# Linear attention, mixture of experts and a squared-ReLU layer on one core: one two-bank tile for the whole kernel, or for the attention stage alone

## The chip, the cores and the metric

The kernel runs on 1 core of one Trainium2 chip. The metric is the device time of one execution in microseconds (us): median 1135.84 over 3 runs (1135.78 to 1138.93). The engines of the core work side by side, each through its own list of instructions in order: PE (TensorE, matmuls; its weight loads are listed as PEld), DVE (VectorE), ACT (ScalarE), POOL (GpSimd) and SP (SyncE, which here only issues DMAs). Where an instruction needs what another engine makes or still reads, it waits for a semaphore, and everything behind it on its own engine waits too.

## The reference

Three layers in a row, on 4 x 576 = 2304 tokens of 512 features:

```python
# 1. linear attention, 8 heads of 64, phi into 2 x 128 features
proj = x @ w_phi;  proj -= max|proj|;  phi = [exp(proj), exp(-proj)]
out  = (phi(q) @ (phi(k)^T v)) / (phi(q) . sum(phi(k)) + 1e-6)
# 2. mixture of 8 experts, two per token, F = 1024
noisy = x @ w_gate + log1p(exp(x @ w_noise)) * noise
y = sum over the top 2 experts e: gate_e * (relu(x @ w1[e]) @ w2[e])
# 3. last layer, F2 = 2048
out = relu(y @ w_in)**2 @ w_out
```

Matrices are multiplied in float32: each product is made of three matmuls (high x high, high x low, low x high), into one PSUM accumulator.

## The kernel before, in words

**Order.** The whole program is written out by hand (`tc.manual_schedule()`): each engine runs its instructions in the order in which the program names them. What the framework adds is the waiting: it records which instruction writes and reads which *tile* and puts a semaphore wait wherever a later one must not overtake an earlier one.

**PSUM.** PE writes into PSUM, 8 banks of 512 float32 per partition. `bank(tag, shape)` hands out a bank by name. `Tk`, `M0`, `M1`, `KV`, `N0` and `N1` are tiles of one bank each, and each call makes a new tile in the bank of that name. `Tq` and `P` are different: they are the two halves of one tile `pair` of two banks, made once at the start, and `bank("Tq")` and `bank("P")` are views of it (`PAIR = ["Tq", "P"]`). In the trace both show as `pair`.

**Attention** (to about 235 us). 36 units run as a software pipeline. `q_b` (L474 on) writes the query projection of a unit into both halves of `pair` at once and copies both out with one ACT instruction (L481); this is why the two banks are one tile. Routing of tokens runs beside it in groups: `r_3b` (L652 on) counts ranks with matmuls into a bank, in the last groups into `P`; `r_4` (L667 on) reads the ranks on DVE, `r_4b` makes the slots, and `r_5` (L742) scatters the token rows into `xg_d` by indirect DMAs from POOL's queue, ordered by expert.

**The seam** (about 235 to 268 us). The first two 128-row blocks of expert 0 ("part 0") are computed while the last routing groups finish. Its accumulators are `ACC[0]` and `ACC[1]`. The last group goes `r_3b(g)`, `e_2(0, 2)`, `r_4(g)`, `r_4b(g)`, `r_5`. When its rows have landed, three blocks `xs` of expert 0 are loaded (L167), transposed (L184), and part 1 begins.

**Experts** (to about 720 us). A part is an expert with its 640 slots (5 blocks j of 128 rows); expert 7 is cut in two parts of 2 and 3 blocks. For each of 8 slices f of F, `e_1(part, f)` makes the hidden slice in `M0` and `M1`, ACT (`hh`, L213) and DVE (`hl`, L210) split it into high and low, and `e_2(part, f)` adds it to five accumulators, one per block: `YP[j] = bank(ACC[j])` with `ACC = ["Tq", "KV", "P", "N0", "N1"]`. `e_1` of the next slice stands before `e_2` of this one. At the border of two experts the order on PE is: the transposes of the next expert's rows (`x_t`, L184) between the blocks of slice 6; slice 7 of blocks 0, 1 and 2; `e_1` of the new expert's slice 0; slice 7 of blocks 3 and 4; `e_1` of its slice 1. After a block's last matmul `e_y` (L220) copies the accumulator to SBUF on ACT and stores it. ACT also converts weights (L138) and, beside DVE and POOL, turns the float64 weights of the last layer into float32 (`wide_a`, `wide_b`, L931 to L945).

**Last layer** (to about 1124 us). Five blocks of rows, four of 4 x 128 and one (the second) of 2 x 128. The first block's rows are gathered and transposed (`l_t`, L988) into the banks `Tk`, `Tq`, `KV` and `M0` just before the last slice of expert 7; DVE and ACT take them out (L95, L96). Then 16 slices per block: `l_1` into `M0` or `M1`, ACT (L1005, L1008) and DVE (L1009, L1010) make the square and split it, `l_2` adds to `bank(ACC[j])`. At the end of a block the accumulators are copied out, j = 0 and 2 by ACT (L1029), j = 1 and 3 by DVE (L1027), and stored. A branch for overfull experts follows; it isn't taken with these inputs.

Of the kernel before, what the change touches and what calls it, by code (L numbers as in the profile page):

```python
# [9 lines left out]
FT = mybir.dt.float32  # L10
# [22 lines left out]
def kernel(  # L33
# [26 lines left out]
    DC = DM // 128  # L60
# [8 lines left out]
    psum = ctx.enter_context(tc.tile_pool(name="psum", bufs=1, space=bass.MemoryType.PSUM))  # L69
# [6 lines left out]
    x_d = dram.tile([NT, DM], FT, name="x_d")  # L76
    g_d = dram.tile([NT, E], FT, name="g_d")

    pair = psum.tile([128, 2, 512], FT, tag="pair", name="pair")

    def bank(tag, shape):
        if tag not in PAIR:
            return psum.tile(shape, FT, tag=tag, name=tag)
        names = "abc"[:len(shape) - 1]
        n = 1
        for x in shape[1:]:
            n *= x
        return pair[:, PAIR.index(tag), :n].rearrange(
            f"p ({' '.join(names)}) -> p {' '.join(names)}", **dict(zip(names, shape[1:])))
# [4 lines left out]
    def hi_lo(hi, lo, src):  # L94
        nc.scalar.activation(hi, src, AF.Copy)  # L95
        nc.vector.tensor_sub(lo, src, hi.bitcast(FT))  # L96
# [46 lines left out]

    NJ = CAP // 128
    NF = F // 128
    ACC = ["Tq", "KV", "P", "N0", "N1"]
    parts = [(0, 0, JA), (0, JA, NJ)] + [(e, 0, NJ) for e in range(1, E - 1)] + [(E - 1, 0, JA), (E - 1, JA, NJ)]
    XG, XT, HT, YP, xp = {}, {}, {}, {}, [None]

# [25 lines left out]
    def x_t(pt, j):  # L175
        e = parts[pt][0]
        if pt not in XT:
            n = RA if pt == 0 else CAP
            XT[pt] = (x_tile(pt, [128, DC, n], FR, "xth", ("kp", 2)), x_tile(pt, [128, DC, n], FR, "xtl", ("kp", 2)))
            if pt == NP - 2:  # L180
                XT[pt + 1] = XT[pt]
        t = bank(["Tk", "M0", "M1"][j % 3], [128, DC, 128])
        for d in range(DC):
            nc.tensor.transpose(t[:, d], XG[pt, j][:, d * 128:d * 128 + 128], ident)  # L184
        c = x_cols(pt, j)
        hi_lo(XT[pt][0][:, :, c], XT[pt][1][:, :, c], t)
# [3 lines left out]
    def e_1(pt, f, later=False):  # L190
        e, j0, j1 = parts[pt]
        wh, wl = wt[2 * e + f // 4, 0]
        fc = (f % 4) * 128
        xh, xl = XT[pt]
        n, x0 = (j1 - j0) * 128, x_cols(pt, j0).start
        if n <= 512:
            cut = [(bank(f"M{f % 2}", [128, n]), 0, n)]
        else:
            cut = [(bank(f"M{i}", [128, n // 2]), i * (n // 2), (i + 1) * (n // 2)) for i in range(2)]
        for d in range(DC):  # L200
            for i, (a, b) in enumerate(((wh, xh), (wh, xl), (wl, xh))):
                for o, c0, c1 in cut:
                    mm(o, a[:, d, fc:fc + 128], b[:, d, x0 + c0:x0 + c1], d == 0 and i == 0, d == DC - 1 and i == 2)
        m = RA if pt == 0 else CAP
        hh = x_tile(pt, [128, m], FR, "hh", ("kth", 2), 2)
        hl = x_tile(pt, [128, m], FR, "hl", ("ktl", 2), 2)
        HT[pt, f] = (hh, hl)

        def low(o, c0, c1):
            nc.vector.scalar_tensor_tensor(hl[:, c0:c1], o, 0.0, hh[:, c0:c1].bitcast(FT), op0=OP.max, op1=OP.subtract)  # L210

        for c in cut:
            nc.scalar.activation(hh[:, c[1]:c[2]], c[0], AF.Relu)  # L213
            if not later:
                low(*c)
        return lambda: [low(*c) for c in cut]
# [6 lines left out]
    def e_2(pt, f, js=None):  # L223
# [4 lines left out]
        for j in range(j0, j1) if js is None else js:  # L228
            if f == 0:
                YP[j] = bank(ACC[j], [128, DM])  # L230
            c = slice((j - j0) * 128, (j - j0) * 128 + 128)
# [5 lines left out]

    with ExitStack() as actx:
        xp[0] = ap_ = actx.enter_context(tc.tile_pool(name="attn", bufs=1))

        KT, KTT, VT, VTT, QT, QTT, NZ = {}, {}, {}, {}, {}, {}, {}

# [545 lines left out]
        for n in range(NU + 2):  # L788
            b, i = divmod(n, 9)
# [97 lines left out]


    wpb[0] = ctx.enter_context(tc.tile_pool(name="wpb", bufs=1))

    with ExitStack() as ectx:
        xp[0] = ep = ectx.enter_context(tc.tile_pool(name="experts", bufs=1))
# [88 lines left out]
        def l_t(m, i):  # L981
            ya, _ = YA.pop((m, i))
            if i == 0:
                X2[m] = [ep.tile([128, DC, 512], FR, name="x2", tag=x, bufs=1)
                         for x in (("xth", "xtl") if m % 2 == 0 else ("xg", "wd"))]
            t = bank("Tk" if m else ("Tk", "Tq", "KV", "M0")[i], [128, DC, 128])
            for d in range(DC):
                nc.tensor.transpose(t[:, d], ya[:, d * 128:d * 128 + 128], ident)  # L988
            c = slice(i * 128, i * 128 + 128)
            hi_lo(X2[m][0][:, :, c], X2[m][1][:, :, c], t)  # L990
# [22 lines left out]
        def l_2(u):  # L1013
# [4 lines left out]
            for j, tt in enumerate(blocks[m]):  # L1018
                if f == 0:
                    OP_[j] = bank(ACC[j], [128, DM])  # L1020
                c = slice(j * 128, j * 128 + 128)
# [114 lines left out]
        for i in range(R):  # L1136
            l_t(0, i)
        e_2(NP - 1, NF - 1)
        NU = len(blocks) * NF2
        for u in range(NU + 1):  # L1140
            m, f = divmod(u, NF2)
            if u < NU:
                l_1(u)
            if u > 0:
                l_2(u - 1)
            if m == 0 and pieces.get((NP, f)):
                ahead_load(2)
                for p in pieces[NP, f]:
                    w_conv(*p)
            if m + 1 < len(blocks):  # L1150
                if f in (3, 6, 9, 12) and f // 3 - 1 < len(blocks[m + 1]):
                    l_gather(m + 1, f // 3 - 1)
                if f in (4, 7, 10, 13) and (f - 1) // 3 - 1 < len(blocks[m + 1]):
                    l_sum(m + 1, (f - 1) // 3 - 1)
                if f in (5, 8, 11, 14) and (f - 2) // 3 - 1 < len(blocks[m + 1]):
                    l_t(m + 1, (f - 2) // 3 - 1)
# [8 lines left out]
    with tc.If(most > CAP):  # L1165
        with ExitStack() as sctx:
# [27 lines left out]
            with tc.For_i(0, NT, 128) as row:  # L1194
# [8 lines left out]
                for e in range(E):  # L1203
# [4 lines left out]
                    for f in range(F // 128):  # L1208
                        t = bank(f"M{f % 2}", [128, 128])
# [3 lines left out]
                    t = bank("P", [128, DM])  # L1213
# [5 lines left out]
                for n in range(F2 // GF):  # L1219
# [4 lines left out]
                    for f in range(GF // 128):  # L1224
                        t = bank(f"M{f % 2}", [128, 128])
# [15 lines left out]
def build(nc, inputs):  # L1241
    import numpy as _np
    import concourse.tile as _tile
    from concourse import mybir as _mybir
    arrays, args = {}, []
    for name in _INS:
        a = _np.ascontiguousarray(inputs[name])
        if a.dtype == _np.float64:
            a = a.view(_np.int64)
        arrays[f"in_{name}_dram"] = a  # L1250
        args.append(nc.dram_tensor(f"in_{name}_dram", a.shape, _mybir.dt.from_np(a.dtype), kind="ExternalInput").ap())
    for i, (shape, dtype) in enumerate(_OUTS):
        dt = _mybir.dt.from_np(_np.dtype(dtype))
        args.append(nc.dram_tensor(f"out_{i}_dram", shape, dt, kind="ExternalOutput").ap())
    with _tile.TileContext(nc) as tc:
        kernel(tc, *args)
    return arrays
# [11 lines left out]
```

## Time and profile before

| | |
|---|---|
| runs: median, lowest, highest | 1135.84, 1135.78, 1138.93 us |
| the profiled execution, and its span from first to last instruction | 1136.58 us, 1134.8 us |
| mean granted TensorE clock | 0.992 |
| busy: PE, PEld | 1095.5 us (97%), 928.2 us (82%) |
| busy: DVE, ACT, POOL | 605.0 us (53%), 478.8 us (42%), 397.6 us (35%) |
| chain that ended last | PE 73%, ACT 2%, DVE 1%, DMA 1% |
| ... by line | PE M L92 36%, PE pair L92 16%, PE N L92 12%, PE KV L92 8% |

Times in a trace count from the span's first instruction. A timeline row gives the start, the duration, the engine, the line, the operation and, as out<-in, the tiles that it writes and reads; a bracket at the end gives the time for which the engine stood idle just before and who ended that. Lines are those of the helper that issues: all matmuls of `mm` have L92, and a tile's name tells them apart. A matmul's duration includes its way through the array, so two that follow each other overlap: what one costs PE is the distance from start to start.

### The profile page before, as it was taken

To read this page: it belongs to the slowest core of one execution; us is meant where nothing else is said; L and a number is where in the kernel's file an instruction comes from. 1 tells how busy PE (TensorE), PEld (TensorE's weight loads), DVE (VectorE), ACT (ScalarE), POOL (GpSimd) and SP (SyncE) were. 2 spreads that over 40 slices of the span, in tenths; PEclk is the share of its full clock that TensorE was granted. 3 is DMA by queue.
4 is the path that set the end of the run, shared out by engine and by line. 5 is a ranking of instruction groups with operands and counts; after the bars stand their busy time and mean duration, and the time that the engine had idled before them with its cause. 6 is when DMAs were issued, how large, how long until landed. Compare 5 with 4: busy or idle time off the path is not lost.

```text
span 1134.8 us, 17634 instructions
## 1 busy us (share of the span) xinstructions
PE 1095.5 (97%) x6652; PEld 928.2 (82%) x6652; DVE 605.0 (53%) x1197; ACT 478.8 (42%) x970; POOL 397.6 (35%) x374
## 2 busy tenths in 40 slices
PE   7999899999999999999999999999999999999996
PEld 5777677698898989898898989788898888888884
DVE  4566677771277767777777773342343333333222
ACT  4666566623434444444435353442232322232221
POOL 3333444654454645454545556461020100000000
PEclk9999999999999999999999999999999999999998
DMA  5777343236564546455554655332121101001001
GB/s 136 231 193 226 95 131 112 95 132 206 169 208 154 188 159 186 171 187 186 186 195 159 208 163 161 114 107 56 38 57 38 30 26 56 19 1 38 1 1 39
DMA packets 105468, 137.77 MB, mean 121 GB/s; under 512 B 17442, under 2 KB 59554, under 8 KB 105378
## 3 DMA queue, kind: packets, MB, share of 16 engines
q1 hardware_dynamic: 99618, 117.72, 32.9%
q0 software_dynamic: 5760, 18.88, 5.1%
q8 instruction: 54, 0.88, 0.3%
q14 instruction: 36, 0.29, 0.1%
HBM read 92.97 MB, written 43.59 MB: 120 GB/s over the span
## 4 chain that ended last, share of the span: by engine, by line
PE 73%; ACT 2%; DVE 1%; DMA 1%; issue 0%; SPq 0%; ACTq 0%
PE M L92 36%; PE pair L92 16%; PE N L92 12%; PE KV L92 8%; PE M L184 1%; PE Tk L184 1%; PE Tk L988 1%; DMA xg_d<-xt,slots 0%; DMA xs<-xg_d 0%; ACT y L220 0%; ACT r L1005 0%; DVE xtl L96 0%; ACT w30h L138 0%; ACT w10h L138 0%; ACT o L1029 0%
## 5 line engine op out<-in xcount | busy, mean ns | idle before, releaser
L1009 DVE TENSOR_TENSOR r<-M,r 128x512 f32<-128x512 f32 (+1 forms) x80 | 51.1, 638 | 247.3 <-ACT h2h L1008 247.3
L213 ACT ACTIVATE hh<-M 128x320 fp32r<-128x320 f32 (+2 forms) x128 | 50.9, 437 | 233.5 <-PE M L92 233.5
L1005 ACT ACTIVATE r<-M 128x512 f32<-128x512 f32 (+1 forms) x80 | 44.4, 555 | 248.0 <-PE M L92 248.0
L210 DVE SCALAR_TENSOR_TENSOR hl<-M,hh 128x320 fp32r<-128x320 f32 (+2 forms) x128 | 58.3, 487 | 123.7 <-ACT hh L213 123.4
L483 POOL PARTITION_ALL_REDUCE qmx<-ps x36 | 69.8, 1941 | 121.4 <-ACT ps L481 100.7
L970 POOL DMA_INDIRECT ya<-y_d,yrows x18 | 18.0, 998 | 188.8 <-PE Tk L988 113.3
L92 PE MATMUL N<-kvc,qp 128*128 128x81 f32 x512 | 65.7, 283 | 5.1 <-DVE ll L519 2.5
L92 PEld LDWEIGHTS N<-kvc,qp 128*128 128x128 f32 x512 | 61.4, 197 | 10.8 <-issue 5.5
L1010 DVE TENSOR_TENSOR h2l<-r,h2h 128x512 fp32r<-128x512 f32 (+1 forms) x80 | 57.7, 721 | 7.3 <-DVE r L1009 0.5
L96 DVE TENSOR_TENSOR ktl<-Tk,kth 128x512 fp32r<-128x512 f32 (+1 forms) x38 | 25.2, 664 | 53.5 <-ACT kth L95 53.5
L1008 ACT ACTIVATE h2h<-r 128x512 fp32r<-128x512 f32 (+1 forms) x80 | 47.1, 589 | 2.6
L92 PE MATMUL M<-x,w30h 128*128 128x512 f32 (+1 forms) x160 | 45.9, 371 | 0.0
L139 POOL TENSOR_TENSOR w20l<-wstage,w20h 128x512 fp32r<-128x512 f32 x20 | 28.1, 1406 | 50.4 <-ACT w20h L138 25.5
L92 PE MATMUL M<-x,w20h 128*128 128x512 f32 (+1 forms) x160 | 45.7, 370 | 0.0
L92 PE MATMUL M<-x,w10h 128*128 128x512 f32 (+1 forms) x160 | 45.7, 370 | 0.0
L92 PE MATMUL M<-x,w00h 128*128 128x512 f32 (+1 forms) x160 | 45.4, 368 | 0.0
L139 POOL TENSOR_TENSOR w30l<-wstage,w30h 128x512 fp32r<-128x512 f32 x20 | 27.4, 1370 | 51.1 <-ACT w30h L138 50.9
L742 POOL DMA_INDIRECT xg_d<-x,slots x32 | 32.9, 1027 | 15.6 <-DVE slots L703 9.4
L139 POOL TENSOR_TENSOR w10l<-wstage,w10h 128x512 fp32r<-128x512 f32 x16 | 22.2, 1390 | 40.2 <-ACT w10h L138 37.1
L940 POOL TENSOR_TENSOR wd<-wd 128x256 f32<-128x256 f32 x32 | 23.9, 746 | 35.3 <-DVE wd L936 34.6
L940 POOL TENSOR_TENSOR wx<-wx 128x256 f32<-128x256 f32 x32 | 23.7, 741 | 35.2 <-DVE wx L936 33.8
L92 PE MATMUL KV<-kp,vt 128*64 128x256 f32 x256 | 35.1, 395 | 0.3 <-ACT kvz L454 0.3
(385 smaller groups left out, 3402.9 us busy)
## 6 DMA issues: line engine op xcount, KB each, us to landing
wstage<-in_moe_w_dram SPq DMA_DIRECT2D x128, 256.0 KB, 3.7
xg_d<-zero SPq DMA_DIRECT2D x8, 1280.0 KB, 7.2
y_d<-y SPq DMA_DIRECT2D x40, 256.0 KB, 2.4
xg<-xg_d SPq DMA_DIRECT2D x7, 1280.0 KB, 6.8
wide<-in_moe_w_in_dram SPq DMA_DIRECT2D x32, 256.0 KB, 3.3
wide<-in_moe_w_out_dram SPq DMA_DIRECT2D x32, 256.0 KB, 2.9
kt<-in_k_dram SPq DMA_DIRECT2D x16, 256.0 KB, 4.2
vt<-in_v_dram SPq DMA_DIRECT2D x16, 256.0 KB, 3.3
```

The costliest lines, as they stand in the source:

```text
L92: nc.tensor.matmul(o, l, r, start=start, stop=stop, skip_group_check=True)
L96: nc.vector.tensor_sub(lo, src, hi.bitcast(FT))
L139: (nc.gpsimd if n >= 2 else nc.vector).tensor_sub(lo[:, c], src, hi[:, c].bitcast(FT))
L210: nc.vector.scalar_tensor_tensor(hl[:, c0:c1], o, 0.0, hh[:, c0:c1].bitcast(FT), op0=OP.max, op1=OP.subtract)
L213: nc.scalar.activation(hh[:, c[1]:c[2]], c[0], AF.Relu)
L483: nc.gpsimd.partition_all_reduce(mx, ps, 128, bass.bass_isa.ReduceOp.absmax)
L742: st = nc.gpsimd.indirect_dma_start(out=xg_d, out_offset=bass.IndirectOffsetOnAxis(ap=slots[:, T0[g] + i, c:c + 1], axis=0), in_=src, in_o ...
L940: nc.gpsimd.tensor_mul(part, part, exp)
L1005: nc.scalar.activation(r[:, :n], t[:, :n], AF.Relu)
L1008: nc.scalar.activation(hh[:, :n], r[:, :n], AF.Square)
L1009: nc.vector.tensor_mul(r[:, :n], t[:, :n], r[:, :n])
L1010: nc.vector.tensor_sub(hl[:, :n], r[:, :n], hh[:, :n].bitcast(FT))
```

## The change

The tile `pair` now lives in a PSUM pool of its own, `ppsum`, which ends with the attention stage. After it a pool `pbank` takes its two banks, `pair` is `None`, and `bank("Tq")` and `bank("P")` make a tile of one bank each, as for the other names. The list of accumulators puts `N0` first and `Tq` fourth, so that part 0, which still runs inside the attention stage, uses `N0` and `KV`. The first block of the last layer transposes into `N0` where it used `Tq`. `q_b` and `r_3b` are as before, and no instruction is added, removed or put elsewhere in the order.

```diff
-    pair = psum.tile([128, 2, 512], FT, tag="pair", name="pair")
+    pair = None
+    pbank = psum

     def bank(tag, shape):
         if tag not in PAIR:
             return psum.tile(shape, FT, tag=tag, name=tag)
+        if pair is None:
+            return pbank.tile(shape, FT, tag=tag, name=tag)
...
-    ACC = ["Tq", "KV", "P", "N0", "N1"]
+    ACC = ["N0", "KV", "P", "Tq", "N1"]
...
         xp[0] = ap_ = actx.enter_context(tc.tile_pool(name="attn", bufs=1))
+        ppsum = actx.enter_context(tc.tile_pool(name="ppsum", bufs=1, space=bass.MemoryType.PSUM))
+        pair = ppsum.tile([128, 2, 512], FT, tag="pair", name="pair")
...
     wpb[0] = ctx.enter_context(tc.tile_pool(name="wpb", bufs=1))
+    pair = None
+    pbank = ctx.enter_context(tc.tile_pool(name="pbank", bufs=1, space=bass.MemoryType.PSUM))
...
-            t = bank("Tk" if m else ("Tk", "Tq", "KV", "M0")[i], [128, DC, 128])
+            t = bank("Tk" if m else ("Tk", "N0", "KV", "M0")[i], [128, DC, 128])
```

## Rows read from the trace of the kernel before

**Rows 1.** The page's first line: the span of the profiled execution.
```profile
span 1134.8 us, 17634 instructions
```
**Rows 2.** Two stretches: length, then PE, PEld, DVE, ACT, POOL busy, PEclk, DMA, GB/s.
```profile
421.00:480.00 59.00, 58.15 (x332) 52.50 (x332) 43.45 (x72) 26.04 (x62) 29.54 (x26) 1.00 0.57 183
...
1124.00:1135.00 11.00, 0.00 (x0) 0.00 (x0) 0.84 (x3) 0.00 (x0) 0.00 (x0) 0.62 0.21 72
```
**Rows 3.** PE's waits: engine, line, releaser: us in total, times, longest.
```profile
PE pair L92 <- ACT y L220: 8.7, 6, 1.5
```
**Rows 4.** Timeline of one expert border, 419 to 422 us, PE and ACT.
```profile
419.15 0.39 PE L92 MATMUL KV<-w11l,hh 128*128 128x512 f32 x1
419.38 0.40 PE L92 MATMUL KV<-w11h,hl 128*128 128x512 f32 x1
...
420.60 0.58 ACT L220 ACTIVATE y<-pair 128x512 f32<-128x512 f32 x1
421.08 0.59 ACT L220 ACTIVATE y<-KV 128x512 f32<-128x512 f32 x1
...
421.23 0.50 PE L92 MATMUL pair<-w11h,hh 128*128 128x512 f32 x1 [1.45 <-ACT y L220]
421.56 0.39 PE L92 MATMUL pair<-w11l,hh 128*128 128x512 f32 x1
```
**Rows 5.** Timeline of DVE at the same border, 419 to 429 us.
```profile
419.05 0.69 DVE L96 TENSOR_TENSOR xtl<-M,xth 128x512 fp32r<-128x512 f32 x1 [0.45 <-ACT xth L95]
...
423.29 0.29 DVE L936 TENSOR_SCALAR wx<-wx 128x256 int32<-128x256 int32 x1
426.07 0.89 DVE L210 SCALAR_TENSOR_TENSOR hl<-M,hh 128x320 fp32r<-128x320 f32 x2 [2.49 <-ACT hh L213]
...
428.45 1.43 DVE L936 TENSOR_SCALAR wd<-wd 128x256 int32<-128x256 int32 x1
```
**Rows 6.** Timeline: transposes then matmul at 656 us; start of the last layer, 717 us.
```profile
656.18 0.60 PE L184 MATMUL M<-ident,xg 128*128 128x128 f32 x4
...
656.53 0.48 PE L92 MATMUL pair<-w11h,hh 128*128 128x512 f32 x1
...
717.08 0.60 PE L988 MATMUL M<-ident,ya 128*128 128x128 f32 x4
...
718.38 0.50 PE L92 MATMUL pair<-w31h,hh 128*128 128x512 f32 x1 [0.70 <-DVE x L96]
...
718.84 0.68 DVE L96 TENSOR_TENSOR x<-M,x 128x512 fp32r<-128x512 f32 x1
...
720.56 0.62 PE L92 MATMUL M<-x,w00h 128*128 128x512 f32 x2
```
**Rows 7.** Timeline of PE at two block ends of the last layer.
```profile
946.89 0.39 PE L92 MATMUL KV<-w31h,h2l 128*128 128x512 f32 x1
...
947.75 0.50 PE L92 MATMUL pair<-w31h,h2h 128*128 128x512 f32 x1 [0.48 <-ACT o L1029]
...
1121.83 0.40 PE L92 MATMUL KV<-w31h,h2l 128*128 128x512 f32 x1
...
1122.22 0.50 PE L92 MATMUL pair<-w31h,h2h 128*128 128x512 f32 x1
```
**Rows 8.** Timeline of the seam: the last routing group, and part 1's start.
```profile
248.68 0.27 PE L92 MATMUL pair<-rt_mask,onesb 128*128 128x16 bf16 x5
...
249.36 0.39 PE L92 MATMUL pair<-w01h,hl 128*128 128x512 f32 x1
...
249.79 0.18 DVE L671 TENSOR_TENSOR rt_rk<-pair,runs 128x24 f32<-128x24 f32 x1 [1.67 <-PE pair L92]
...
251.66 0.96 POOL L742 DMA_INDIRECT xg_d<-x,slots  x1 [2.36 <-DVE slots L703]
...
263.71 0.66 PE L184 MATMUL M<-ident,xs 128*128 128x128 f32 x4 [0.60 <-DMA xs<-xg_d]
...
267.41 0.41 PE L92 MATMUL M<-xth,w00h 128*128 128x384 f32 x1 [1.46 <-DVE xtl L96]
```

## The prediction

> **What bounds the kernel now.** The first view to read is the page: the span is 1134.8 us [rows 1], and the profiled execution took 1136.58 us, so 1.8 us lie around the span and no step below touches them. The second is the table of stretches. In the stretch of one expert PE is busy for 58.15 of 59.00 us, at a granted clock of 1.00, that is 2.4 GHz [rows 2]; DVE, the next engine, for 43.45. PE sets the time, so an edit pays only where it takes idle time from PE, or lets the data for which PE waits come sooner. The third view is therefore PE's waits. The largest group after the start is one that a reader can't explain by data: matmuls into `pair` wait for the ACT copy `y`, 6 times, 8.7 us in all [rows 3]. The fourth is the timeline there. PE ends its matmuls into `KV` (block 1) and wants `pair` (block 2, the half `P`). It starts 0.05 us after ACT's copy of `pair` ends (420.60 + 0.58 = 421.18, start 421.23) [rows 4]. That copy reads block 0, the half `Tq`: another bank than the one PE writes. Meanwhile ACT reads `KV` from 421.08 to 421.67, and PE's start at 421.23 doesn't care for that [rows 4]. So what holds PE is not a copy out of PSUM as such but a copy out of the same tile: the framework orders a write to one half behind a read of the other. The change makes two tiles of the halves from the experts on.
>
> **The change part by part.** It adds no instruction and moves none; it moves accumulators between banks and takes away waits. I go through every place where one half of `pair` waits for the other.
>
> *1. Expert borders, six.* Matmuls into one accumulator start 0.23 us apart (419.15, 419.38) [rows 4]. Without the wait the first into `P` would start at 419.38 + 0.23 = 419.61; it starts at 421.23, 1.62 us late. The one behind it follows after 0.33 us instead of 0.23 (421.23, 421.56) [rows 4], since PE's pipeline is empty: another 0.10. One border costs 1.72 us, six (the count of [rows 3]) 10.3 us. ACT's order there stays, so the copy of block 0 stays as late as it is, but no matmul waits for it until slice 0 of the new expert reaches that accumulator, two `e_1` later.
> What is late next: `e_1` of the new expert would start at 420.3, and needs the last transposed rows; DVE ends those at 419.05 + 0.69 = 419.74 [rows 5], 0.5 us before. Then `M0` and `M1` must be emptied before the second `e_1`, which stands only two groups behind the first. DVE's `hl` starts at 426.07 now, would be wanted at 424.35, and DVE's last work before it ends at 423.29 + 0.29 = 423.58 [rows 5]: 0.77 us to spare. Both covers hold, so I take the whole 1.72.
>
> *2. Start of the last layer, once.* The transposed rows in `Tq` are read by DVE and the matmuls into `P` wait for it, 0.70 us [rows 6]. A matmul behind four transposes starts 0.35 us after their start where nothing holds it (656.18, 656.53); here it is 718.38 - 717.08 = 1.30 [rows 6]: 0.95 us saved. Next late would be `l_1` into `M0`, now at 720.56, then at 719.61; DVE empties `M0` at 718.84 + 0.68 = 719.52 [rows 6]. It fits by 0.09, so the bounds are 0.7 and 0.95, and I take 0.95.
>
> *3. Block ends of the last layer, four.* The same pattern with the ACT copy `o`. The long form is 947.75 - 946.89 - 0.23 + 0.10 = 0.73 us, twice; the short form, at the ends of the first and of the last block, 1122.22 - 1121.83 - 0.23 + 0.10 = 0.26 us, twice by this row [rows 7]. The block of two row tiles uses no `P`. Sum 2.0 us.
>
> *4. The seam, once.* Here the false order runs the other way, and no PE wait shows it. `r_3b` ends its rank matmuls in `P` at 248.68 + 0.27 = 248.95; the next instructions of PE are block 0 of part 0, into `Tq`, to 249.36 + 0.39 = 249.75; DVE reads the ranks at 249.79 after 1.67 us of idling for `pair` [rows 8]. A read of `P` waits for the later write to `Tq`. With part 0 on `N0` it can start at 248.99: 0.80 us sooner. Behind it stand the slots, POOL's scatter (which waits 2.36 us for the slots), its landing, the load `xs`, and PE, which idles 0.60 us for `xs` and 1.46 us for the split rows [rows 8]. POOL's scatters are paced by each other from there, so all moves by 0.80, and PE has the idle time to take it: 0.8 us, bounds 0 (if landing times eat it) and 0.8.
>
> *5. New accumulators.* `N0` in part 0 was last read by the normalisation of an attention unit, and two whole `e_1` of part 0 stand on PE between that unit's matmuls and the first write; nothing to pay. `Tq` as the fourth accumulator and the new tiles per call follow the pattern of `KV`, `N0` and `N1`, which shows no wait of its own in [rows 3]. The pool border needs the last reader of the old tile, DVE's ranks at 250 us [rows 8], 20 us before an expert writes there. Each costs 0.
>
> Sum: 10.3 + 0.95 + 2.0 + 0.8 = 14.05 us. From the profiled 1136.58 that gives 1122.5; the median of the runs stands 0.74 lower, at 1135.84, which gives **1121.8 us**.
>
> **The rivals.**
> *A. DVE takes the wait over.* The 0.77 us of cover in part 1 rests on three short DVE operations, and the same operation that takes 0.29 us there takes 1.43 us at 428.45 [rows 5], while POOL works on weights. If one of the three before `hl` is stretched by 1.14 us, each border gives back 0.37 us, 2.2 in all: 1124.0, inside my range. If two are, 1.51 each, 9.1 in all: 1130.9. For it: DVE is the second busiest engine. Against it: at the border DVE's and POOL's work is released by ACT's conversions, which PE's earlier start doesn't move.
> The Trainium skill, SBUF — State Buffer, section Who interferes with whom, has a rule that speaks for A: a DVE operation with two SBUF inputs, or in a two-port mode, and a GpSimd operation that reads SBUF exclude each other for the whole instruction. By that rule the stretch is a whole POOL operation each time one is under way, so it would be 1130.9 if POOL's conversions reached these three; the trace's 0.29 and 1.43 [rows 5] agree with the rule, and by the rule `hl` itself, with one input from PSUM, is never stretched.
> *B. The change doesn't do what it says*: the two tiles of `pbank` are still ordered as one, the waits of [rows 3] stay, and it takes 1135.8. Against it: `KV` beside `pair` [rows 4].
> *C. The pool border drains the core (slower).* The new pool may hand out its banks only when the whole of what was there before is done on every engine, once at the seam and once where the branch at the end uses the pool's tiles. The nearest row for a stop of all engines is the end of the kernel, where PE does nothing for 11 us and the clock goes to 0.62 on average [rows 2]. One such stop gives 1121.8 + 11 = 1132.8, two 1143.8; it makes the kernel slower from 14 us of stops on. Against it: pools of SBUF change at the same place now, and PE's only stops there are data, 0.60 and 1.46 us [rows 8].
>
> **How the numbers follow.** The forecast has 0.83: its own range is 1120.3 to 1125, below the value if idle time is worth a little more than the start distances say, above it if parts 2 and 4 fail (1.75) or one DVE operation is stretched (2.2). A with two operations 0.07, B 0.05, C 0.05 in all (0.02 with one stop, 0.03 with two). The range of 8 in 10 is 1119.8 to 1126.5; it leaves out B, C and the far end of A. A measurement of this kernel tells about 0.3% from no change, that is 3.4 us: faster is everything below 1132.4. That is the forecast and A, 0.90; same holds B and C with one stop, 0.07; slower is C with two stops, 0.03.
>
> **What would show it.** In the profile after, PE's wait for `y` should be gone and matmuls into `P` follow those into `KV` after 0.23 us (step 1); the distance from one expert's border to the next should shrink by 1.7 us. No wait for `o` or for DVE's `x` should stand ahead of `P` (steps 2, 3). DVE's rank read should start within 0.1 us of the end of `r_3b`, and PE's two idle times at the seam should shrink by 0.8 us together (step 4). It is wrong if that distance stays (B), if a wait of `M` for `hl` appears behind each border (A), or if PE stops for several us near 270 us with the first write of `P` (C).

## The result, and the profile after

The changed kernel took 1122.01 us (median; 1119.29 to 1123.73), beside it the kernel before 1135.81 (1134.30 to 1138.93): ratio 0.987, interval 0.984 to 0.990. The forecast was 1121.8. The sum came out, but not every term of it, and part of that is luck. The profiled execution took 1123.73 us; its span [rows 1]:

```profile
span 1122.0 us, 17634 instructions
```

The lines of the changed kernel are 3 to 7 higher than before (`mm` is L95, `e_y` L223). PE's waits, the longest of them (engine, line, releaser: us in all, times, longest). `pair <- ACT y` [rows 3] is gone; a wait for `o` or for DVE's `x` is not in the list either:

```profile
PE Tk L371 <- DMA ktt<-in_k_dram: 5.7, 1, 5.7
PE Tk L376 <- DVE ktl L99: 2.6, 2, 1.7
PE N L95 <- DVE ll L524: 2.5, 2, 1.8
PE M L95 <- DVE xtl L99: 2.2, 2, 1.5
PE N L95 <- ACT kvc L474: 2.1, 2, 1.6
PE M L187 <- DMA xs<-xg_d: 0.9, 1, 0.9
PE N L95 <- DVE h2l L1017: 0.7, 1, 0.7
```

The same border as in [rows 4], timeline of PE and ACT:

```profile
417.81 0.40 PE L95 MATMUL KV<-w11h,hl 128*128 128x512 f32 x1
...
418.05 0.39 PE L95 MATMUL P<-w11h,hh 128*128 128x512 f32 x1
418.28 0.40 PE L95 MATMUL P<-w11l,hh 128*128 128x512 f32 x1
...
418.51 0.39 PE L95 MATMUL P<-w11h,hl 128*128 128x512 f32 x1
...
418.74 0.45 PE L95 MATMUL M<-xth,w20h 128*128 128x320 f32 x2
...
419.04 0.58 ACT L223 ACTIVATE y<-N 128x512 f32<-128x512 f32 x1
```

`P` follows `KV` after 0.24 us instead of 1.85, and PE is in the next expert's `e_1` before ACT begins to copy block 0. The copy is as late as ever (it starts 1.23 us behind the last matmul into `KV`, 1.22 before); nobody waits for it. The table of stretches, one expert and two pieces around part 1 (columns as in [rows 2]), shows PE without a gap in the expert:

```profile
418.74:476.61 57.87, 57.87 (x334) 52.56 (x332) 44.10 (x72) 26.55 (x64) 30.18 (x27) 1.00 0.58 187
...
260.00:280.00 20.00, 16.96 (x78) 15.14 (x78) 3.74 (x6) 7.70 (x14) 7.63 (x6) 0.83 0.66 209
280.00:300.00 20.00, 20.00 (x108) 17.98 (x107) 3.84 (x7) 7.81 (x16) 10.13 (x8) 1.00 0.61 195
```

To find where 12.8 us of span went, I cut both timelines at the same instructions of PE:

| piece | before | after | difference | forecast |
|---|---|---|---|---|
| start to the last `r_3b` | 248.68 | 245.78 | -2.90 | 0 |
| last `r_3b` to part 1's first matmul | 18.73 | 19.65 | +0.92 | -0.8 |
| part 1, to the first matmul of expert 1 | 35.31 | 37.47 | +2.16 | 0 |
| experts 1 to 6, six periods | 357.70 | 347.33 | -10.37 | -10.3 |
| expert 7, to the last layer's first matmul | 60.14 | 59.56 | -0.58 | -0.95 |
| last layer, to its last matmul | 402.93 | 400.80 | -2.13 | -2.0 |
| tail | 11.31 | 11.41 | +0.10 | 0 |

The last three of PE's pieces, all behind part 1, give 13.08 us where the forecast had 13.25. I measure every kernel below by that distance too (first matmul of expert 1 to the last matmul of PE: 820.77 before, 807.69 after), because it repeats: 807.60 to 807.71 in all profiles of kernels with these accumulators as separate tiles. Of the first three rows the forecast had only the -0.8 of step 4, which came out the other way. The three add up to nearly nothing (+0.18), and that is luck.

### The profile page after: what moved, and what is told of

Read it like the earlier page. It is cut to its first block, busy times and chain, and to the rows that moved or that the text cites. A ratio compares the mean times of both kernels' runs of the same rounds, so it can differ in the third digit from the quotient of the medians.

```text
span 1122.0 us, 17634 instructions
## 1 busy us (share of the span) xinstructions
PE 1091.3 (97%) x6652; PEld 927.6 (83%) x6652; DVE 605.3 (54%) x1197; ACT 477.6 (43%) x970; POOL 397.0 (35%) x374
## 4 chain that ended last, share of the span: by engine, by line
PE 73%; DVE 1%; DMA 1%; ACT 0%; issue 0%; POOL 0%; SPq 0%; POOLq 0%
PE M L95 36%; PE N L95 12%; PE KV L95 8%; PE Tq L95 8%; PE P L95 8%; PE M L187 1%; PE Tk L187 1%; PE Tk L995 1%; DMA xg_d<-xt,slots 0%; DMA xs<-xg_d 0%; DVE wd L951 0%; DVE xtl L99 0%; DVE wx L951 0%; ACT xth L98 0%; DVE h2l L1017 0%
## 5 line engine op out<-in xcount | busy, mean ns | idle before, releaser
L95 PE MATMUL N<-kvc,qp 128*128 128x81 f32 x512 | 65.6, 283 | 5.2 <-DVE ll L524 2.5
L95 PEld LDWEIGHTS N<-kvc,qp 128*128 128x128 f32 x512 | 61.4, 196 | 10.8 <-issue 5.5
L95 PE MATMUL M<-x,w30h 128*128 128x512 f32 (+1 forms) x160 | 45.9, 371 | 0.0
L95 PE MATMUL M<-x,w20h 128*128 128x512 f32 (+1 forms) x160 | 45.7, 370 | 0.0
L95 PE MATMUL M<-x,w10h 128*128 128x512 f32 (+1 forms) x160 | 45.7, 370 | 0.0
L95 PE MATMUL M<-x,w00h 128*128 128x512 f32 (+1 forms) x160 | 45.4, 368 | 0.0
L952 DVE SCALAR_TENSOR_TENSOR wd<-wd 128x256 f32<-128x256 f32 x32 | 35.1, 1096 | 1.1
```

The source lines that it names most:

```text
L95: nc.tensor.matmul(o, l, r, start=start, stop=stop, skip_group_check=True)
L952: nc.vector.scalar_tensor_tensor(exp, ok, TINY * TINY, exp, op0=OP.is_ge, op1=OP.mult)
```

## The experiments

The medians below stand beside runs of the kernel before on the same chip; the ratio is to those. "Landing" is the distance from the issue of the last scatter (POOL, `xg_d<-xt`) to the issue of the first load `xs` (SP), which waits for it. In the edits, `warm(tag, k, w, x)` puts `k` matmuls that nobody reads into the bank `tag`, and `...` stands for lines left out.

**1. The order of accumulators alone.** One tile `pair` for the whole kernel, but its halves on blocks 2 and 3 instead of 0 and 2; at a border a whole `e_1` of the new expert lies between these two:

```diff
-    ACC = ["Tq", "KV", "P", "N0", "N1"]
+    ACC = ["N0", "KV", "P", "Tq", "N1"]
...
-            t = bank("Tk" if m else ("Tk", "Tq", "KV", "M0")[i], [128, DC, 128])
+            t = bank("Tk" if m else ("Tk", "N0", "KV", "M0")[i], [128, DC, 128])
```

> One two-bank tile for the whole kernel, as before; only the accumulators take the new order (N0, KV, P, Tq, N1) and the first transposes of the last layer use N0. Theory T (a write to one half of a tile waits for a read of the other half that stands before it in the program): the halves now belong to blocks 2 and 3. At the expert borders a whole e_1 stands between them, so no wait: all of 10.3 us is saved, 0.95 at the start of the last layer and 0.8 at the seam too. But where blocks 2 and 3 follow each other directly (the four ends of four-tile blocks in the last layer, and the last slice of expert 7) the matmuls into Tq wait for the copy of P, some 1.1 us each, 5.5 in all: 5.5 us above the changed kernel, 1127.5 us. Rival S (the split of the tile is what pays, whatever the order): the border waits stay, about 1135. Rival O (the order alone pays): as the changed kernel, 1122, with no wait in the last layer.

1127.94 us (1126.14 to 1131.13), ratio 0.9916 [0.9896, 0.9936]; from expert 1 on 812.58. Its waits for `pair`:

```profile
PE pair L92 <- ACT o L1029: 2.8, 4, 0.7
...
PE pair L92 <- ACT y L220: 1.0, 2, 0.7
```

The theory's 1127.5 came out. The six border periods are all gone down to those of the changed kernel (57.89 on average), though the tile is still one: block 3 still has to wait for the copy of block 2, but ACT makes that copy beside the `e_1`. In the last layer nothing lies between the two, and four block ends now pay 0.7 each, where before two paid 0.48, and expert 7 takes 60.66. So the order alone gives 8.2 of 13.1 us, and the split on top of it 4.9 more.

**2. The split alone, with the old order.** The changed kernel with the accumulators of before from part 1 on, and the old bank for the last layer's first transposes (`ACC0` serves part 0, so that the seam is as changed):

```diff
-    ACC = ["N0", "KV", "P", "Tq", "N1"]
+    ACC = ["Tq", "KV", "P", "N0", "N1"]
+    ACC0 = ["N0", "KV"]
...
-                YP[j] = bank(ACC[j], [128, DM])
+                YP[j] = bank((ACC0 if pt == 0 else ACC)[j], [128, DM])
...
-            t = bank("Tk" if m else ("Tk", "N0", "KV", "M0")[i], [128, DC, 128])
+            t = bank("Tk" if m else ("Tk", "Tq", "KV", "M0")[i], [128, DC, 128])
```

> The changed kernel with its separate tiles, but from part 1 on with the old order of accumulators (Tq, KV, P, N0, N1) and the old banks for the first transposes of the last layer; part 0 stays on N0 and KV. T: with separate tiles the order is of no weight: 1122 us as the changed kernel, matmuls into P 0.23 us behind those into KV at each border. Rival O (the order pays): back to about 1135 less the seam's 0.8, with the border waits of 1.45 us.

1126.80 us (1122.03 to 1127.88), ratio 0.9892 [0.9870, 0.9913]; from expert 1 on 807.65, the changed kernel's value. Separate tiles take the wait away in the old order too. The median is 4.8 us above the 1122 that was expected; in the profile, the longest of its six runs, the excess lies ahead of expert 1, which starts at 307.0 us (302.90 in the changed kernel's), with the granted clock at 0.74 in 220 to 240 us and at 0.91 in 260 to 280.

**3. The false order made worse.** One tile, and its halves on blocks 0 and 1, which follow each other at the border (part 0 as in experiment 2):

```diff
-    ACC = ["Tq", "KV", "P", "N0", "N1"]
+    ACC = ["Tq", "P", "KV", "N0", "N1"]
+    ACC0 = ["N0", "KV"]
...
-                YP[j] = bank(ACC[j], [128, DM])
+                YP[j] = bank((ACC0 if pt == 0 else ACC)[j], [128, DM])
...
-            t = bank("Tk" if m else ("Tk", "Tq", "KV", "M0")[i], [128, DC, 128])
+            t = bank("Tk" if m else ("Tk", "Tq", "M1", "M0")[i], [128, DC, 128])
```

> The kernel before, with one two-bank tile, but its halves are given to blocks 0 and 1 (order Tq, P, KV, N0, N1); part 0 on N0 and KV, third transpose of the last layer in M1. T: block 1 now stands directly behind block 0, so one group of matmuls (0.69 us) less covers the wait for the copy of block 0: 6 x 0.69 = 4.1 us more at the borders, about 0.69 more at each of four block ends of the last layer and about 0.95 at the end of the two-tile block, 3.7 in all; the start of the last layer loses its 0.95 wait and the seam its 0.8: 1135.8 + 4.1 + 3.7 - 1.75 = 1141.9 us, with the border wait at about 2.1 us instead of 1.45. Rival (the wait is for ACT being late, not for a shared tile): 1135 to 1136, with the wait ahead of block 2 as before.

1151.81 us (1148.71 to 1158.36), ratio 1.0134 [1.0106, 1.0162]; from expert 1 on 836.88. The sign is right, the size is not: 10 us more than forecast. Waits of PE, and two stretches of the table:

```profile
PE pair L92 <- ACT y L221: 13.5, 7, 2.1
...
PE pair L92 <- ACT o L1030: 4.9, 5, 1.2
```

```profile
400.00:420.00 20.00, 20.00 (x117) 17.87 (x117) 14.63 (x24) 8.65 (x20) 8.15 (x8) 1.00 0.52 168
420.00:440.00 20.00, 17.86 (x95) 15.85 (x94) 13.26 (x21) 10.12 (x23) 9.65 (x8) 0.91 0.51 165
```

Each border wait is 2.14 us long now, and behind five of the six the granted clock of the 20 us is 0.91: 3.4 us of them run at 1.2 GHz instead of 2.4, 17 us in all five. In the kernel before, a wait of 1.45 us [rows 4] left the clock at 1.00 [rows 2], six times of six.

**4. The same, with the stop filled.** To see whether the clock is the missing 10 us: seven matmuls into `Tk`, which nobody reads, behind block 0 at each border.

```diff
             if last and pt > 0:
                 e_y(e, j)
+            if last and j == 0 and 0 < pt < NP - 2:
+                warm("Tk", 7, wh[:, 0, :128], wh[:, 0])
```

> The kernel with the halves on blocks 0 and 1 (1151.8 us, 10 more than forecast, with the granted clock at 0.91 in five 20 us slices behind borders), and seven unread matmuls into Tk at each border behind block 0, 1.6 of the 2.1 us for which PE stands there. Theory: the missing 9 us were the clock, which falls to half behind a stop of 2.1 us and does not behind one of 1.45; with the stop filled the clock stays at 1.00 behind the borders and the time comes to the forecast 1141.9, up to 1143.5. Rival: the stop itself is longer than forecast by 1.5 us a border; then filling changes nothing, 1151.

1146.54 us (1142.54 to 1150.85), ratio 1.0087 [1.0060, 1.0114]; from expert 1 on 829.08, that is 7.8 less than experiment 3 for 42 matmuls more. Waits of PE and a stretch behind a border:

```profile
PE pair L92 <- ACT y L227: 3.9, 7, 0.7
```

```profile
420.00:440.00 20.00, 19.46 (x112) 17.29 (x111) 14.16 (x22) 10.65 (x23) 9.88 (x9) 1.00 0.51 165
```

The clock stays at 1.00 and a period takes 60.28 us (the first 60.41), where it took 60.64 to 62.18 (mean 61.55). So these stops cost more than their length: the half clock behind them too. 17 us at half clock cost at most 8.5, which fits the 7.8 given back. The rest of the miss isn't the borders' clock: by the forecast's own terms the distance from expert 1 on would be 820.77 + 4.1 + 3.7 - 0.95 = 827.6, 1.5 less than was measured, and some 3 us lie ahead of expert 1, where part 1 took 37.66. The median missed its 1143.5 by 3.

**5. The seam alone.** The kernel before, with part 0 on `N0` and `KV` (`ACC0` as in experiment 2, nothing else).

> The kernel before with one edit: block 0 of part 0 accumulates in N0, so that no write to Tq stands between the last rank matmuls and DVE's read of them. T: DVE reads the ranks within 0.1 us of their last matmul and the last scatter is issued 0.8 us sooner, counted from those matmuls; if the landing times follow, PE's idle times at the seam shrink by 0.8 us and the kernel takes 1135.0 us. Rival (the seam is set by the landing of the scatter, which varies by as much): 1135.8, no difference that can be measured.

1137.52 us (1133.36 to 1140.41), ratio 1.0006 [0.9990, 1.0022]; from expert 1 on 820.74, as before. DVE reads the ranks 0.31 us after the start of `r_3b`'s count, so the false order is gone there too. Yet the landing is 4.47 us instead of 3.20, and part 1 takes 37.69 instead of 35.31. No gain of step 4 is shown; the runs can't rule out its 0.8 us either, which would be a ratio of 0.9993.

**6. The changed kernel again**, beside experiments 7 and 8.

> The changed kernel again, for a second profile and more runs beside the three below. From the first matmul of expert 1's part to the last matmul it should again take 807.7 us (13.1 less than before), whatever the time of the whole; what lies ahead of that should vary by some us with the granted clock at 120 to 160, 220 to 240 and 260 to 280 us. 1120 to 1126 us.

1122.01 us (1119.44 to 1125.89), ratio 0.9872 [0.9848, 0.9897]; from expert 1 on 807.60; landing 4.22, part 1 36.88 us.

**7. The seam's stop filled.** The changed kernel with 3, 1 and 5 unread matmuls into `N1` around the transposes of part 1:

```diff
...
+        hw = wt[0, 0][0]
         for j in range(JA, NJ):
+            warm("N1", (3, 1, 0)[j - JA], hw[:, 0, :128], hw[:, 0])
             x_t(1, j)
+        warm("N1", 5, hw[:, 0, :128], hw[:, 0])
```

> The changed kernel with nine matmuls that nobody reads at the seam, where PE waits for the rows of expert 0 (three before the first block's transposes, one before the second, five after the last; they write the idle bank N1). Theory: at the seam the length of PE's stop decides whether the granted clock falls to half for the first matmuls of part 1, which cost 2.2 us in the profile of the changed kernel (part 1 took 37.5 us against 35.3). With the stop filled, part 1 takes 35.3 us in every profile and the median falls by 1 to 2 us beside the changed kernel run with it. Rival: the clock follows something else, part 1 is as often 37.5 us, and the nine matmuls cost up to 0.5 us.

1126.25 us (1120.19 to 1126.99), ratio 0.9890 [0.9862, 0.9918]. The part that it aims at does what was said: part 1 takes 35.32 us at a granted clock of 1.00. The landing stays late, 4.53. The median is 4 us above experiment 6 instead of 1 to 2 below: this profile has 0.69 in 140 to 150 us and 0.75 in 230 to 240, in the attention stage, which the edit doesn't touch. That forecast failed on what varies from run to run there.

**8. Four stops of the attention stage filled as well**, with 12, 5, 3 and 12 short matmuls into `Tk`:

```diff
...
+            if n in (35, 37):
+                warm("Tk", 3 if n == 35 else 12, wsh, wbh)
             if 0 <= n - QC < NU:
                 q_d(n - QC)
+            if n in (20, 21):
+                warm("Tk", 12 if n == 20 else 5, wsh, wbh)
```

> The same with fillers also at the four longest waits of PE in the attention stage (12, 5, 3 and 12 short matmuls into Tk in slots 20, 21, 35 and 37, where PE waits 1.8, 0.7, 0.5 and 1.6 us). Theory: the lower clock at 120 to 160 and 220 to 240 us is the after-effect of those waits; the part 1 of the profile starts at 262 to 263 us at a clock of 1.00 all through, the mean clock is 0.997 or more and the runs of this kernel lie at 1117 to 1119 us, closer together than those of the others. Rival: no difference to the kernel with the seam alone.

1121.50 us (1119.78 to 1124.77), ratio 0.9876 [0.9853, 0.9899]: no better than experiment 6 by the runs, and above the forecast 1117 to 1119. Its profile has the clock at 1.00 through the attention stage, as the theory said, but experiments 9 and 12, which fill the same stops, have falls to half near 131 and 141 us again. So the theory isn't borne out. But the landing fell to 2.77 us, which filling the seam alone (experiment 7) had not done. What differs is a DMA of 16 KB in the queue "instruction", a fetch of code; that it is PE's is inferred from its moving with PE's instructions. Here it starts at 249.25 us, 4.7 us ahead of the last scatter's issue; in experiments 5 to 7 it lies upon the scatter.

**9. The attention stops alone, and 10. the same 32 matmuls where they fill no stop** (four in each of slots 5 to 12), to move that fetch and nothing else. Experiment 9's edit is the one above; that of experiment 10:

```diff
...
+            if 5 <= n < 13:
+                warm("Tk", 4, wsh, wbh)
             if 0 <= n - QC < NU:
                 q_d(n - QC)
```

> The changed kernel with 32 short matmuls into Tk, whose results nobody reads, at four stops of PE in the attention stage (12, 5, 3 and 12 of them); nothing is added at the seam. Open is why the last scatter's rows come about a microsecond later in the changed kernel (4.4 us from the last scatter's issue to the first xs issue, 3.2 before). Theory: one 16 KB instruction fetch of PE lies on a DMA engine while the last scatter runs; 32 more PE instructions ahead of the seam bring it about 5 us sooner, as where seam and attention were filled. Then the distance is 2.6 to 3.2 us, PE's stop at the seam stays under 2.6 us in all, and the clock behind it stays at 1.00, so that part 1 takes 35.3 us without any filling of the seam. Rival: the landing has to do with the sooner scatter itself; then it stays at 4.2 to 4.6, the clock is at half for a while and part 1 takes 36.9 to 37.7. Both: first matmul of expert 1's part to the last PE matmul 807.7 us. Median by the theory 1120 to 1122, by the rival 1121 to 1123.5.

> The changed kernel with the same 32 short matmuls, four behind each other in slots 5 to 12 of the attention pipeline, where they fill none of the four stops. This moves the instruction fetch alone. Theory of the fetch: it comes about 5 us sooner against the last routing group, the distance from the last scatter's issue to the first xs issue is 2.6 to 3.2 us, part 1 takes 35.3 us at a clock of 1.00. Rival: 4.2 to 4.6 us and 36.9 to 37.7 us. By both the dips of the clock in the attention stage stay, and the matmuls cost up to 3.5 us where PE is the bound there (0.1 us each); 807.7 us from expert 1 to the last PE matmul. Median 1120 to 1125.

These two ran where the kernel before took 1149.20 us (1144.96 to 1150.33): 1134.68 (1130.79 to 1136.63), ratio 0.9867 [0.9841, 0.9894], and 1137.87 (1137.42 to 1140.24), ratio 0.9914 [0.9894, 0.9934]. The medians forecast for them don't apply there; the distances do. The landing is 2.77 us in both, part 1 takes 35.30 and 35.32 us at a clock of 1.00, with nothing filled at the seam. But in these two the last scatter wasn't sooner, for a reason that stays open: it came 9.00 and 9.31 us behind `r_3b`, 9.32 before and 8.50 in the changed kernel. So they don't put out the rival (the sooner scatter itself); experiments 8 and 12 do, with the scatter 8.51 and 8.48 us behind `r_3b` and a landing of 2.77 and 2.83. The DMA view of the landing, from the last scatter's issue to the `xs` issue in 40 slices, in the changed kernel:

```profile
GB/s 0 0 262 337 561 374 262 449 150 0 0 0 0 0 449 374 299 449 374 299 38 0 0 0 37 0 37 0 37 37 0 37 37 0 37 0 0 0 0 0
...
q8 instruction: 1, 0.02, 2.5%
```

and the same of experiment 9:

```profile
GB/s 2 0 0 0 527 351 468 351 410 351 293 468 176 351 14 10 7 0 0 0 0 0 468 351 468 351 351 468 293 468 351 176 0 0 0 0 0 0 0 0
```

The scatter's data are there in two bursts in both. In the changed kernel a trickle of 37 GB/s in single slices follows: over a slice of 0.109 us that is 4 KB, one packet at a time, after the bulk has landed. The fetch is one packet, and 2.5% of 16 engines over 4.38 us is 1.75 us on one engine: the packets that stand behind it there come last. In experiment 9 no fetch is in the window, and no trickle behind the bulk. The trace doesn't name the engines, but its packets fit one queue: counted from the scatter's issue, the fetch lasts from 0.51 to 2.25 us, the next packet of 4 KB starts at 2.23, eight follow one another to 3.88, mostly 0.16 us each, and the load is issued 0.50 us later. The bulk had ended at 2.34. In experiment 9 the last packet ends at 2.36.

**11 and 12. The changed kernel and experiment 9 on one chip.**

> The changed kernel once more, as it is, beside the next one. First matmul of expert 1's part to the last PE matmul 807.7 us; the last scatter's landing 4.2 to 4.4 us with the instruction fetch in it, part 1 between 36.8 and 37.5 us, some of it at half clock. Ratio to the kernel before 0.987.

> The changed kernel with the 32 unread matmuls at the four stops of the attention stage once more, now timed beside the changed kernel itself. Theory (the fetch out of the landing's way, a shorter stop, full clock in part 1): landing 2.6 to 3.2 us, part 1 35.3 us, so 1.6 to 2.2 us of part 1 and 1.0 to 1.6 us of the landing are won; the matmuls themselves lie in stops. That would be 1 to 3 us below the changed kernel's median. Rival: the attention stage gives it back, by the matmuls or by a clock that falls elsewhere; then the medians are within 1 us.

1124.06 us (1120.55 to 1127.53), ratio 0.9899 [0.9874, 0.9923], and 1122.52 (1120.34 to 1123.31), ratio 0.9869 [0.9843, 0.9894]. The intervals overlap: the version with unread matmuls isn't shown to beat the changed kernel. In experiment 12 the landing is 2.83 and part 1 35.28, as forecast. In experiment 11 the profile differs from what was expected: landing 3.55, part 1 35.28 without half clock. So the changed kernel has executions that don't pay for the half clock.

Over all twelve profiles and the two of the result:

| where the 16 KB fetch lies | the fetch takes | landing | part 1 |
|---|---|---|---|
| 4.6 to 5.0 us ahead of the last scatter's issue (experiments 8, 9, 10, 12) | 1.10 to 1.66 | 2.77 to 2.83 | 35.28 to 35.32 |
| upon it, landing under 4 us (before, experiments 1, 3, 11) | 0.93 to 1.00 | 3.20 to 3.81 | 35.28 to 35.31 |
| upon it, landing over 4 us, seam not filled (after, experiments 2, 4, 5, 6) | 1.27 to 1.95 | 4.22 to 4.64 | 36.85 to 37.69 |
| the same, seam filled (experiment 7) | 1.97 | 4.53 | 35.32 |

## Why the prediction was right, step by step

**The false order as the cause**: shown from both sides. With two tiles it goes in the old order as in the new (experiment 2), with one tile it goes where the halves are used far apart (experiment 1) and grows where they are neighbours (experiments 3 and 4). Rival B is out, and so is rival C: no stop of PE lies at the first write of `P` (271.86 us), and PE's only waits at the seam are for data.

**Step 1** (10.3): 10.37. The period, from one expert's first `e_1` to the next one's, fell from 59.60 to 57.87 (the row 418.74:476.61 above), by 1.73 for 1.72 forecast; the kernel before in the table of stretches:

```profile
422.02:481.62 59.60, 58.15 (x333) 52.50 (x332) 44.05 (x72) 26.64 (x62) 30.14 (x27) 1.00 0.56 181
```

The covers held: no wait of `M` for `hl` stands behind a border of these six.

**Step 2** (0.95, bounds 0.7 to 0.95): the piece gave 0.58, below its bounds. At the place itself the step was right [rows 6]; timeline of the changed kernel:

```profile
707.29 0.60 PE L995 MATMUL M<-ident,ya 128*128 128x128 f32 x4
...
707.65 0.48 PE L95 MATMUL P<-w31h,hh 128*128 128x512 f32 x1
...
709.06 0.68 DVE L99 TENSOR_TENSOR x<-M,x 128x512 fp32r<-128x512 f32 x1
...
709.79 0.72 PE L95 MATMUL M<-x,w00h 128*128 128x512 f32 x2
```

0.36 us from transposes to `P` instead of 1.30, and DVE ends with `M0` at 709.74, 0.05 us ahead of `l_1`. What it gives back is lost earlier in the same part, and that is rival A in small, at one place that I had not looked at:

```profile
664.40 1.47 POOL L142 TENSOR_TENSOR w00l<-wstage,w00h 128x512 fp32r<-128x512 f32 x1
...
664.76 1.40 DVE L952 SCALAR_TENSOR_TENSOR wd<-wd 128x256 f32<-128x256 f32 x1
...
665.99 0.40 PE L95 MATMUL N<-w31l,hh 128*128 128x512 f32 x1
...
666.08 0.74 DVE L213 SCALAR_TENSOR_TENSOR hl<-M,hh 128x256 fp32r<-128x256 f32 x2
...
666.54 0.50 PE L95 MATMUL N<-w31h,hl 128*128 128x512 f32 x1 [0.15 <-DVE hl L213]
666.88 0.40 PE L95 MATMUL KV<-w31h,hh 128*128 128x512 f32 x1
```

In the kernel before the same two operations lay the other way round, and `wd` took 0.42 us:

```profile
674.27 0.42 DVE L945 SCALAR_TENSOR_TENSOR wd<-wd 128x256 f32<-128x256 f32 x1
...
674.33 1.52 POOL L139 TENSOR_TENSOR w00l<-wstage,w00h 128x512 fp32r<-128x512 f32 x1 [0.37 <-ACT w00h L138]
```

Now POOL's `w00l` is under way when `wd` starts, `wd` takes 1.40 us, `hl` queues behind it, and the matmul on `hl` and the one behind it start 0.55 and 0.34 us after the one ahead of them, for 0.23 each: 0.43 lost. The part takes 59.54 to 59.58 us in every profile of this kernel, with unread matmuls or without. The cover was worked out for slice 0 of the new expert, not for the later slices.

**Step 3** (2.0): 2.13. At the block end of [rows 7] `P` now follows `KV` at once:

```profile
935.90 0.39 PE L95 MATMUL KV<-w31h,h2l 128*128 128x512 f32 x1
936.13 0.39 PE L95 MATMUL P<-w31h,h2h 128*128 128x512 f32 x1
```

**Step 4** (0.8): failed, as "all moves by 0.80, and PE has the idle time to take it". The scatter moved; its landing and PE did not follow. The seam of the changed kernel, for [rows 8]:

```profile
245.78 0.27 PE L95 MATMUL pair<-rt_mask,onesb 128*128 128x16 bf16 x5
...
246.08 0.18 DVE L676 TENSOR_TENSOR rt_rk<-pair,runs 128x24 f32<-128x24 f32 x1 [0.86 <-PE pair L95]
...
247.95 0.97 POOL L747 DMA_INDIRECT xg_d<-x,slots  x1 [1.58 <-DVE slots L708]
...
254.28 0.96 POOL L747 DMA_INDIRECT xg_d<-xt,slots  x1 [0.22 <-issue]
...
258.66 1.28 SPq L170 DMA_DIRECT2D xs<-xg_d  x3
...
261.13 0.65 PE L187 MATMUL M<-ident,xs 128*128 128x128 f32 x4 [0.92 <-DMA xs<-xg_d]
262.44 0.66 PE L187 MATMUL Tk<-ident,xs 128*128 128x128 f32 x4 [0.66 <-DMA xs<-xg_d]
...
265.43 0.66 PE L95 MATMUL M<-xth,w00h 128*128 128x384 f32 x1 [1.46 <-DVE xtl L99]
265.89 0.52 PE L95 MATMUL M<-xtl,w00h 128*128 128x384 f32 x1
266.21 0.52 PE L95 MATMUL M<-xth,w00l 128*128 128x384 f32 x1
```

From `r_3b` to the rank read 0.30 us instead of 1.11, and POOL waits 0.78 us less: that is the 0.8, and it reaches the last scatter (8.50 us behind `r_3b`, before 9.32). Then the landing takes 4.38 instead of 3.20 us, and from the first `xs` issue to part 1 another 0.56 us are lost (6.77 for 6.21). The other profiles take 6.36 to 7.01 there, all longer than the one of before; why wasn't settled. PE idles 0.92 and, for the second block, 0.66 us for `xs` instead of 0.60 and 0.28. Then comes what no case of mine had: part 1's matmuls start 0.32 us apart (before 0.175), at 1.2 GHz, until the clock comes back; 2.2 us. A likely account of the later landing is that the sooner scatter brings itself further under the fetch of PE's code, whose moment PE's own progress sets. It isn't shown: with the fetch starting 0.79 us behind the issue in both, the changed kernel landed once after 4.22 us and once after 3.55 (experiments 6 and 11), where the fetch itself took 1.59 and 1.00.

The forecast also counted too much idle time. The 1.46 us for the split rows are the way from the last transposes over ACT and DVE to `e_1`. They stand at 1.46 in eleven of the fourteen profiles, however soon the rows land (1.78 in experiment 10, less only where the seam is filled). PE could give up only the waits for `xs`, 0.88 us in all before. Experiment 12 shows what that is worth with the fetch out of the way: from `r_3b` to part 1 17.96 us for 18.73, with no wait left ahead of the first transposes. Of those 0.77 us some belong to the landing, 0.37 sooner there than before; what step 4 gives by itself can't be told apart.

**Step 5** (0): right; no new wait on `N0`, `Tq` or at the pool border.

**The total** came out right because 2.90 us in the attention stage, whose order and tiles are the same in both kernels, stood against step 4 and the half clock. That is luck of the execution. The profile of before runs at 1.2 GHz until 17.4 us, and at 130.0 to 133.4, 140.3 to 143.7 and 229.0 to 232.4; that of after until 10.8 us and at 222.4 to 229.2. PE's lead in the profile of after grows where the other is slow, to 1.3 us by 17 us and 4.3 by 144, and falls back to 2.9. The last `r_3b` lies anywhere from 245.8 to 251.2 us in profiles without unread matmuls in the attention stage. In the runs the mean granted clock goes with the time (0.997 at 1119.29 us, 0.990 at 1123.73), so this is the likely reason why the runs of one kernel spread by some 3 to 7 us. What decides in which execution the clock falls there wasn't settled. What is shown for the change is the 13.1 us from expert 1 on; the rest of the 13.8 between the medians is within the spread.

## What to carry to other kernels

Where PE waits for a copy out of a bank that it doesn't write, look for one tile over both; split it where the shared access ends, or, if it can't be split, give its parts to uses far apart in the order, which here won 8.2 of 13.1 us with one list and one name. Work out a stop's price from its length and from the granted clock behind it. When an engine is moved ahead against others, check the cover in every slice that follows, not in the first alone. Before an idle time is counted as room, ask what fills it: waiting for data that may come sooner, or a chain of copies that stays as long.

## What the runs showed of the hardware

- Behind a stop of PE of 1.45 us at a border the granted clock stayed at 1.00 (six of six); behind stops of 2.14 us it fell to half in five of six. Seven unread matmuls in the stop kept it at 1.00 and saved 1.25 us per expert net.
- A fetch of 16 KB of instructions lasted 0.9 to 2 us as one packet. Scatters that were under way then landed 0.4 to 1.9 us later (3.20 to 4.64 for 2.77 us), with two to eight of their 4 KB packets one behind another at the end. 32 unread matmuls more, in either of two places ahead, moved the fetch by about 5 us against `r_3b`.
- A DVE operation on weights that took 0.42 us in the kernel before took 1.40 in the changed one, where a POOL operation of 1.47 us was under way as it started.
